# Product of w3 and w_out started with four row blocks on four accumulators, with another order of loads and a pace taken from what is left

## Chip, cores and metric

The kernel runs on one core of one Trainium2 chip. The metric is the device time of one execution in microseconds (us). Inputs are what the reference's `setup_inputs` draws; arrays stay in HBM until the kernel loads them.

## What is computed

```python
attn_out = softmax(rmsnorm(q) @ rmsnorm(k).T / 8) @ v      # 4 batches, 12 heads, 448 rows, 64 columns
x = attn_out.transpose(0, 2, 1, 3).reshape(1792, 768)
h = (x @ w1) * (x @ w2) @ w3                               # w1, w2: 768 x 1024; w3: 1024 x 1024
x = h @ w_out                                              # w_out: 1024 x 768
h = x @ w_in                                               # w_in: 768 x 2048
x = (h * clip(h + 3, 0, 6) / 6) @ w_out2                   # w_out2: 2048 x 768
```

The two products with w3 and w_out in a row have no nonlinear step between them, so the kernel multiplies w3 by w_out once, at its start, and the first block's last two products become one with the 1024 x 768 result.

## The kernel before

The program has three stages that overlap.

1. **Attention.** Heads are taken in 24 pairs, six pairs to a batch. A main loop of about 216 steps (eight steps to a pair) issues, in each step, one score product (two reduced-precision fp32 products of 448 columns, L627 and L628), its scaling and maximum on VectorE (L634), the exponential of the step before on ScalarE (L646), four transposes of an older step (L653), their copies into high and low parts (L662 on ScalarE, L672 on VectorE), and the product of transposed probabilities with V (L701 in fp32 for the first two pairs, L705 and L706 after them). L627 occurs 192 times and serves here as the step's mark.
2. **Filler.** Into each step `fill(us, aux)` puts other products worth `us` of TensorE time, taken from the generator `products()`: first `wprime()` (the product of w3 and w_out), then for each of the four batches `layer1` (L391, L396) and `layer2` (L88 to L90). `rate(t)` gives the share for step `t`. If a product's operands are not prepared the generator yields `None`, and the step goes on without it.
3. **The second block** (w_in, w_out2), a long stretch of products from L1242 and L1304, starts when the filler has ended.

`wprime()` computes 8 x 2 x 8 products of 128 x 384: for row block `a` of w3 (8), half `n` of w_out's columns (2) and inner block `c` (8). One accumulator (one PSUM bank) gathers the eight products of one `(a, n)`; `evac` copies it into a high part on ScalarE and a low part on VectorE and stores six small pieces to HBM, where `layer2` reads them back. Accumulators come from `bank(tag)`: four tags, `s` (scores), `t` (transposes), `v` (product with V) and `f` (filler), with two banks each.

The weights arrive as 64-bit floats, in half blocks: 512 KB for a half row block of w3 (kind `a`, 512 columns), 384 KB for a half block of w_out (kind `c`) and of the first layer's weights (kind `l`). All go through four `raw` buffers. `convert` makes fp32 of one: two ScalarE instructions (L148, L149) and one on VectorE (L151). A converted w3 half takes one of eight `w3` buffers, which are given back by `W["free"]` after the products of the second column half. The list `order` in `open_wprime` says in which order the half blocks are loaded and converted; `Prep` converts them one after another, up to three us' worth in each step, and no further than the buffers reach. Before the main loop the first twelve are converted, between the loads and first steps of the attention, and `fill(8.0, 0.0)` issues eight us of products.

The program is written in this order and a scheduler then places the instructions on each engine. All loads and stores go through SP's queue, in order. `issue_after` ties a load or a filler to an older instruction.

## Time and profile before

| | us |
|---|---|
| runs shown | 1142.69, 1149.24, 1151.27 |
| their median | 1149.24 |
| the profiled execution | 1141.81 |
| its span, first to last instruction | 1140.0 |

The rows further down come from the profiled execution. Times in it count from its first instruction. A timeline row gives the start, the time from the first of its merged instructions to the end of the last, the engine, the line, the operation, the tiles (written <- read) and how many there are; in brackets stands the engine's idle time before it with what ended it. An fp32 product shows as two records, a reduced-precision one as one. A product's record lasts longer than the distance to the next one's start, since products are pipelined. A row of the windows gives a stretch, its length, then for each engine its busy time with the number of instructions in brackets, at the end the granted clock of TensorE as a share of full speed, the mean busy share of the 16 DMA engines, and what they moved. A row of the waits gives the total, the number and the longest. A row of groups gives count, busy time and mean duration in ns, and the idle time before. "PE" is TensorE, "PEld" its weight loads, "DVE" VectorE, "ACT" ScalarE, "POOL" GpSimd.

### The profile page before, as it was taken

The page shows a single profiled execution, that of the slowest core. Times are in us where ns is not written, and L with a number is a line of the kernel's source. Part 1 is how long each engine was busy: PE and PEld are TensorE (multiplying, and loading weights), DVE is VectorE, ACT ScalarE, POOL GpSimd, SP SyncE. Part 2 cuts the span into 40 slices and gives each one's busy share as a digit, 9 for nine tenths or more (in the row PEclk, how much of TensorE's full clock was granted, in tenths as well). Part 3 has the DMA queues.
Part 4 walks back from the last instruction along what each step waited for, and adds up shares of the span by engine and source line. Part 5 has one row for each costly group of instructions (what it writes and reads, how often), then busy time and mean ns, then how long its engine had stood idle before and what let it go on. Part 6 is the DMA issues. An engine that isn't in the chain of part 4 may idle for free.

```text
span 1140.0 us, 17361 instructions
## 1 busy us (share of the span) xinstructions
PE 1103.1 (97%) x5483; PEld 944.0 (83%) x5483; DVE 850.8 (75%) x1927; ACT 812.4 (71%) x1729; POOL 177.9 (16%) x156
## 2 busy tenths in 40 slices
PE   5999999999999999999999999999999999999998
PEld 3545666788887888888888899899989989999998
DVE  5757988779866888778753225999988998887764
ACT  6989778899758878787754433766666776666764
POOL 1133223554322213221102000000000000000000
PEclk9999999999999999999999999999999999999999
DMA  8999655689889988997789998665469955434972
GB/s 267 331 317 342 213 171 164 243 293 377 272 279 316 308 295 269 336 342 253 232 287 324 382 362 299 217 214 200 164 228 362 389 172 168 153 117 160 335 264 74
DMA packets 109660, 299.04 MB, mean 262 GB/s; under 512 B 13280, under 2 KB 46048, under 8 KB 109568
## 3 DMA queue, kind: packets, MB, share of 16 engines
q1 hardware_dynamic: 109568, 297.93, 76.2%
q8 instruction: 43, 0.70, 0.3%
q14 instruction: 49, 0.40, 0.1%
HBM read 230.61 MB, written 67.27 MB: 261 GB/s over the span
## 4 chain that ended last, share of the span: by engine, by line
PE 60%; ACT 7%; DMA 7%; DVE 3%; issue 2%; POOL 0%; SPq 0%; ACTq 0%; POOLq 0%; DVEq 0%
PE acc L1304 17%; PE bank L391 10%; PE sB L1242 8%; PE sA L1242 8%; PE bank L396 5%; DMA rsb<-rsd 2%; PE bank L653 2%; ACT PP L646 1%; PE bank L88 1%; PE bank L89 1%; PE bank L90 1%; PE bank L627 1%; PE bank L628 1%; PE bank L706 1%; DMA raw<-in_wo_dram 1%
## 5 line engine op out<-in xcount | busy, mean ns | idle before, releaser
L1304 PE MATMUL acc<-g,wt 128*128 128x448 f32 x1008 | 211.7, 366 | 1.2 <-ACT g L1192 1.0
L1304 PEld LDWEIGHTS acc<-g,wt 128*128 128x128 f32 x1008 | 188.9, 188 | 17.7 <-ACT g L1192 1.9
L391 PE MATMUL bank<-xhl,ws 128*128 128x448 f32 x768 | 180.5, 367 | 1.6 <-ACT bs L367 1.3
L391 PEld LDWEIGHTS bank<-xhl,ws 128*128 128x128 f32 x768 | 143.5, 188 | 15.1 <-ACT bs L367 1.8
L634 DVE CUSTOM_DVE_ANT_0 PP<-bank,rb,rq 112x448 f32<-112x448 f32 x192 | 128.7, 675 | 27.4 <-PE bank L628 21.1
L646 ACT ACTIVATE PP<-PP,mx 112x448 f32<-112x448 f32 x192 | 127.5, 665 | 28.1 <-DVE mx L641 24.3
L1242 PE MATMUL sA<-xo,wt 128*128 128x448 f32 x504 | 112.0, 366 | 1.1 <-ACT u L1253 1.1
L1242 PE MATMUL sB<-xo,wt 128*128 128x448 f32 x504 | 112.2, 367 | 0.8 <-ACT u L1253 0.6
L252 PE MATMUL bank<-woh,w 128*128 128x384 f32 x256 | 97.6, 509 | 14.6 <-DVE woh L151 10.9
L1242 PEld LDWEIGHTS sB<-xo,wt 128*128 128x128 f32 x504 | 94.4, 188 | 9.9 <-ACT u L1253 1.9
L1242 PEld LDWEIGHTS sA<-xo,wt 128*128 128x128 f32 x504 | 94.6, 188 | 9.6 <-ACT u L1253 1.5
L662 ACT ACTIVATE xh<-bank 128x448 fp32r<-128x448 f32 (+1 forms) x156 | 83.1, 539 | 24.6 <-PE bank L653 20.5
L653 PEld LDWEIGHTS bank<-ident,PP 112*128 112x128 f32 x672 | 78.8, 141 | 23.9 <-issue 6.1
L1011 DVE TENSOR_TENSOR wt<-wf,wt 128x384 fp32r<-128x384 f32 x160 | 87.3, 555 | 15.1 <-ACT wt L1010 14.9
L672 DVE TENSOR_TENSOR xl<-bank,xh 128x448 fp32r<-128x448 f32 x142 | 87.4, 617 | 11.5 <-ACT xh L662 10.1
L653 PE MATMUL bank<-ident,PP 112*128 112x112 f32 x672 | 94.1, 261 | 1.5 <-DVE xl L672 1.1
L396 PE MATMUL bank<-xhl,ws 128*128 128x448 f32 x384 | 94.5, 366 | 0.0
L252 PEld LDWEIGHTS bank<-woh,w 128*128 128x128 f32 x256 | 48.9, 196 | 43.7 <-DVE woh L151 13.4
L148 ACT ACTIVATE raw<-raw 128x384 f32<-128x384 f32 (+1 forms) x112 | 63.8, 569 | 28.6 <-DMA raw<-in_wo_dram 11.6
L1010 ACT ACTIVATE wt<-wf 128x384 fp32r<-128x384 f32 x160 | 80.4, 517 | 4.8 <-PE acc L1304 2.7
L151 DVE SCALAR_TENSOR_TENSOR raw<-raw 128x384 int32<-128x384 int32 x80 | 48.9, 613 | 46.0 <-ACT raw L149 38.8
L627 PE MATMUL bank<-K,Q 128*112 128x448 f32 x192 | 77.7, 407 | 1.5 <-DVE mx L634 1.4
(134 smaller groups left out, 2110.3 us busy)
## 6 DMA issues: line engine op xcount, KB each, us to landing
ws<-w12d SPq DMA_DIRECT2D x48, 768.0 KB, 6.2
ws<-wpd SPq DMA_DIRECT2D x32, 768.0 KB, 6.5
wf<-wfd SPq DMA_DIRECT2D x56, 384.0 KB, 5.6
raw<-in_wo_dram SPq DMA_DIRECT2D x44, 384.0 KB, 5.8
td<-G SPq DMA_DIRECT2D x32, 448.0 KB, 2.5
G<-td SPq DMA_DIRECT2D x32, 448.0 KB, 6.2
raw<-in_w_dram SPq DMA_DIRECT2D x32, 384.0 KB, 6.9
w12d<-ws SPq DMA_DIRECT2D x16, 768.0 KB, 5.9
```

The source lines that it names most:

```text
L252: nc.tensor.matmul(ps[:, :NH], W["w3"][a, c // 4][:, cs], W["woh"][c, n], start=c == 0, stop=c == M1 - 1)
L391: nc.tensor.matmul(ps[:, :S], w[:, 0, ks], x[:, y, :], start=k == 0 and y == 0, stop=False)
L396: nc.tensor.matmul(ps[:, :S], w[:, 1, ks], L["xhl"][i][:, 0, :], start=False, stop=k == KD - 1)
L627: nc.tensor.matmul(ps[:CP, :S], qs, k1[:, j, :], start=True, stop=False)
L634: anchors[8 * i + s].append(nc.vector.tensor_tensor_reduce(out=T["PP", i][:, c, sl], in0=ps[:CP, :S], in1=T["rb", i][:, sl], op0=ALU.mult, ...
L646: anchors[8 * i + s].append(nc.scalar.activation(v, v, AF.Exp, bias=T["m", i][:, 8 + s : 9 + s], accum_out=T["sum", i][:, s : s + 1]))
L653: nc.tensor.transpose(ps[:, c * CP : c * CP + CP], src[:, c, kb * P : kb * P + P], ident[:CP, :CP])
L662: nc.scalar.activation(hi, ps, AF.Copy)
L672: nc.vector.tensor_sub(lo, ps, hi)
L1011: nc.vector.tensor_sub(t[:, 1, :], src, t[:, 0, :])
L1242: mm = nc.tensor.matmul(ps[:, :S], w[:, a, ks], x[:, c, :], start=first and k == 0 and n == 0, stop=k == KD // 2 - 1 and n == 2, skip_grou ...
L1304: nc.tensor.matmul(ps, w[:, y, ns], x[:, z, :], start=first and a == 0, stop=end and a == 2, skip_group_check=h in "674")
```

## The change

The first pass takes four row blocks of w3 with the first half of w_out's columns on four accumulators, two of them with tag `f` and two with tag `v`; two passes of two row blocks follow with the second half; the other four row blocks stay as they were. The load order brings the halves of row blocks 2 and 3 ahead. During `wprime` the rate is the product's remaining time over the steps left to step 58, at least 4.0 us over them, in place of 1.3 us per step, and `spent` counts the filler from the start.

```diff
-        halves = [(a, h) for a in range(2, M1) for h in range(2)]
-        order = [("a", 0, 0), ("c", 0, 0), ("a", 1, 0)] + [("c", c, 0) for c in range(1, 4)] + [("a", 0, 1), ("a", 1, 1)]
+        halves = [(a, h) for a in range(4, M1) for h in range(2)]
+        order = [("a", 0, 0), ("c", 0, 0), ("a", 1, 0)] + [("c", c, 0) for c in range(1, 4)]
+        order += [("a", 2, 0), ("a", 3, 0)] + [("a", a, 1) for a in range(4)]
         order += [("c", c, 0) for c in range(4, M1)] + [("c", c, 1) for c in range(M1)]
...
-        for group in [(0, 1)] + [(a,) for a in range(2, M1)]:
-            for n in range(2):
-                acc = [bank("f") for _ in group]
-                for c in range(M1):
-                    for a, ps in zip(group, acc):
-                        while not ready(a, n, c):
-                            yield None
-                        mul(a, n, c, ps)
-                        yield 0.73
-                    if n == 1 and c % 4 == 3:
-                        W["free"] += len(group)
+        passes = [((0, 1, 2, 3), 0), ((0, 1), 1), ((2, 3), 1)] + [((a,), n) for a in range(4, M1) for n in range(2)]
+        for group, n in passes:
+            acc = [bank("fv"[z // 2]) for z in range(len(group))]
+            for c in range(M1):
                 for a, ps in zip(group, acc):
-                    later(evac, a, n, ps)
+                    while not ready(a, n, c):
+                        yield None
+                    mul(a, n, c, ps)
+                    yield 0.73
+                if n == 1 and c % 4 == 3:
+                    W["free"] += len(group)
+            for a, ps in zip(group, acc):
+                later(evac, a, n, ps)
...
             state["debt"] -= c
-            if "pool" in L:
-                state["spent"] += c
+            state["spent"] += c
...
     def rate(t):
         if "pool" not in L:
-            return 1.3, 3
+            return max(2 * M1 * M1 * 0.73 - state["spent"], 4.0) / max(8 * HP + 10 - t, 4), 3
         if L["cur"] < 8:
             return 2.5, 4
-        left = (B - 1) * (2 * M1 * KD * 3 + KD * M1 * 3) * 0.189 - state["spent"]
+        left = 2 * M1 * M1 * 0.73 + (B - 1) * (2 * M1 * KD * 3 + KD * M1 * 3) * 0.189 - state["spent"]
         return max(left - 25.0, 0.0) / max(8 * NP + 14 - t, 1), 2
```

What the scheduler makes of it, first on SP's queue after the load of the first pair's K. `raw<-in_w3t_dram` is a half row block of w3, `raw<-in_wo_dram` a half block of w_out; before:

```order
L99 DMA kr<-in_kT_dram 128x896
L99 DMA raw<-in_w3t_dram 128x1024 x2
L99 DMA raw<-in_wo_dram 128x768 x4
L99 DMA qr<-in_qT_dram 128x896
L99 DMA kr<-in_kT_dram 128x896
L99 DMA raw<-in_wo_dram 128x768 x3
```

and after the change:

```order
L99 DMA kr<-in_kT_dram 128x896
L99 DMA raw<-in_w3t_dram 128x1024 x6
L99 DMA qr<-in_qT_dram 128x896
L99 DMA kr<-in_kT_dram 128x896
L99 DMA raw<-in_wo_dram 128x768 x3
```

Six half blocks of w3 stand in a row where two stood, and the second pair's q and k follow six weight loads as before, with larger loads among them.

On TensorE, around the second four inner blocks (`w_` and a number are w3 halves, each number another buffer; L252 of before is L253 of after); before, two row blocks:

```order
L653 MATMUL bank<-ident,PP 128x112 x2
L252 MATMUL bank<-woh,w_190 128x384
L252 MATMUL bank<-woh,w_196 128x384
L627 MATMUL bank<-K,Q 112x448
L628 MATMUL bank<-K,Q 112x448
```

and after the change, four:

```order
L628 MATMUL bank<-K,Q 112x448
L253 MATMUL bank<-woh,w_206 128x384
L253 MATMUL bank<-woh,w_212 128x384
L253 MATMUL bank<-woh,w_218 128x384
L253 MATMUL bank<-woh,w_242 128x384
L653 MATMUL bank<-ident,PP 128x112 x4
```

Each block of w_out is now followed by four products in place of two.

On TensorE, around the first product with V (L701); before, behind the 16th product of w3 and w_out:

```order
L628 MATMUL bank<-K,Q 112x448
L653 MATMUL bank<-ident,PP 128x112 x4
L701 MATMUL bank<-xh,vo 64x448
L627 MATMUL bank<-K,Q 112x448
L628 MATMUL bank<-K,Q 112x448
```

and after the change, behind the 46th:

```order
L253 MATMUL bank<-woh,w_206 128x384
L253 MATMUL bank<-woh,w_212 128x384
L701 MATMUL bank<-xh,vo 64x448 x3
L253 MATMUL bank<-woh,w_206 128x384
L253 MATMUL bank<-woh,w_212 128x384
L653 MATMUL bank<-ident,PP 128x112 x4
L687 MATMUL bank<-xh,vo 64x448 x2
```

The first product with V has moved behind 30 more products of the filler, and three of them now follow each other.

## Rows read from the trace of the kernel before

**Rows 1.** The page: busy time of each engine, share, instructions.
```profile
PE 1103.1 (97%) x5483; PEld 944.0 (83%) x5483; DVE 850.8 (75%) x1927; ACT 812.4 (71%) x1729; POOL 177.9 (16%) x156
```

**Rows 2.** Windows: busy us of PE, PEld, DVE, ACT, POOL; clock, DMA, GB/s.
```profile
0.00:25.20 25.20, 12.05 (x32) 6.08 (x33) 13.31 (x21) 15.73 (x24) 3.30 (x8) 1.00 0.91 286
25.20:67.00 41.80, 38.05 (x162) 21.96 (x160) 28.57 (x88) 39.67 (x91) 7.14 (x7) 1.00 0.96 303
67.00:130.00 63.00, 60.83 (x240) 36.42 (x241) 44.71 (x116) 56.33 (x124) 21.42 (x19) 1.00 0.94 320
130.00:195.00 65.00, 65.00 (x314) 45.75 (x312) 54.81 (x158) 50.48 (x115) 17.40 (x15) 1.00 0.51 157
195.00:241.00 46.00, 42.72 (x222) 35.85 (x222) 36.52 (x91) 40.62 (x94) 26.74 (x23) 1.00 0.77 261
241.00:298.00 57.00, 57.00 (x310) 49.42 (x309) 48.12 (x119) 52.35 (x117) 25.89 (x23) 1.00 0.95 331
298.00:370.00 72.00, 69.33 (x368) 61.23 (x368) 50.83 (x141) 50.31 (x116) 18.86 (x16) 0.98 0.88 290
```

**Rows 3.** Waits of TensorE between 25.2 and 130 us.
```profile
PE bank L252 <- DVE wst L245: 1.5, 1, 1.5
PE bank L705 <- ACT xh L662: 1.3, 1, 1.3
...
PE bank L628 <- POOL K L608: 0.7, 1, 0.7
```

**Rows 4.** Timeline of TensorE, pieces from 25 to 573 us.
```profile
41.91 0.96 PE L701 MATMUL bank<-xh,vo 128*64 128x448 f32 x2 [0.53 <-DMA vo<-in_v_dram]
...
62.98 0.43 PE L627 MATMUL bank<-K,Q 128*112 128x448 f32 x1
...
66.95 5.40 PE L252 MATMUL bank<-woh,w 128*128 128x384 f32 x16 [1.50 <-DVE wst L245]
72.18 0.55 PE L653 MATMUL bank<-ident,PP 112*128 112x112 f32 x4
...
199.22 0.36 PE L628 MATMUL bank<-K,Q 128*112 128x448 f32 x1
199.42 0.97 PE L391 MATMUL bank<-xhl,ws 128*128 128x448 f32 x4
...
208.56 0.37 PE L627 MATMUL bank<-K,Q 128*112 128x448 f32 x1
...
369.84 0.37 PE L627 MATMUL bank<-K,Q 128*112 128x448 f32 x1
...
572.73 0.36 PE L627 MATMUL bank<-K,Q 128*112 128x448 f32 x1
```

**Rows 5.** ScalarE between 25 and 130 us by form: count, busy us, mean ns.
```profile
L646 ACT ACTIVATE PP<-PP,mx 112x448 f32<-112x448 f32 x36 | 24.2, 675 | 2.2 <-DVE mx L641 2.2
L148 ACT ACTIVATE raw<-raw 128x384 f32<-128x384 f32 x22 | 12.5, 570 | 3.7 <-DMA raw<-in_w_dram 3.7
```

**Rows 6.** DMA issues between 25 and 75 us: count, KB each, us to landing.
```profile
raw<-in_wo_dram SPq DMA_DIRECT2D x10, 384.0 KB, 7.7
```

**Rows 7.** Timeline of ScalarE: four conversions.
```profile
32.95 0.56 ACT L149 ACTIVATE raw<-raw 128x384 int32<-128x384 uint16 x1
...
62.68 0.67 ACT L148 ACTIVATE raw<-raw 128x512 f32<-128x512 f32 x1 [1.21 <-DMA raw<-in_w3t_dram]
...
64.58 0.56 ACT L148 ACTIVATE raw<-raw 128x384 f32<-128x384 f32 x1 [0.68 <-DMA raw<-in_w_dram]
65.04 0.53 ACT L149 ACTIVATE raw<-raw 128x384 int32<-128x384 uint16 x1
...
80.23 0.55 ACT L148 ACTIVATE raw<-raw 128x384 f32<-128x384 f32 x1 [3.00 <-DMA raw<-in_w_dram]
80.69 0.55 ACT L149 ACTIVATE raw<-raw 128x384 int32<-128x384 uint16 x1
```

**Rows 8.** The page, part 5: weight loads of the products of w3 and w_out.
```profile
L252 PEld LDWEIGHTS bank<-woh,w 128*128 128x128 f32 x256 | 48.9, 196 | 43.7 <-DVE woh L151 13.4
```

## Prediction, made before the changed kernel was run

> **What bounds the kernel now.** The page comes first: TensorE is busy 97% of the span, VectorE and ScalarE three quarters of it [rows 1]. A share over 1140 us says little about a change that sits in the first tenth, so the windows by stage come next [rows 2]. Up to 25.2 us (the first score) every engine waits for the first loads and TensorE works 12 us; the change leaves the order of that stretch alone. From 25.2 to 67 us, the head of the attention loop, TensorE is busy 38.05 of 41.80 us, ScalarE 39.67 of 41.80, and the DMA share is 0.96: three resources are near their end at once. From 67 to 130 us TensorE idles 2.2 us, from 130 to 195 us (the rest of the w3 x w_out product) not at all, then 3.3 us around the start of layer 1 and 2.7 us near 350 us. All idle time of TensorE between 25.2 and 370 us is 11.9 us, 1.0% of the span: an ideal rearrangement of everything that the change touches would win that much.
>
> Third, the waits of TensorE between 25.2 and 130 us [rows 3]: seven kinds and 5.6 us in all, three of them shown. The largest is 1.5 us at 66.95 us, where the third accumulator pass waits for the evacuation of the pass before it. No single wait governs the head, and the granted clock is 1.00 in every window here except 0.98 in one [rows 2], so nothing is to be had from the clock.
>
> Fourth, unit prices. Eight fp32 products of 128x384 (16 records) start at 66.95 us and the next instruction at 72.18 us: 0.65 us each [rows 4]. A 448-column product in the reduced format starts 0.20 us after the one before it (199.22 and 199.42 us) [rows 4]. The product of w3 and w_out is 8 x 2 x 8 = 128 such fp32 products, 83 us of TensorE whatever the order.
>
> **What the change does to the work.** It neither removes nor adds arithmetic: 128 products, 32 loads and conversions, 16 evacuations, 96 small stores stay. It moves. Counted in the two orders at the same score instruction: before the 19th score, which comes at 62.98 us now [rows 4], TensorE has 32 of the 128 products behind it in the old order and 48 in the new (16 x 0.65 = 10.4 us more). The lead shrinks to 4 us at the 25th score, since the old order catches up there with a block of products, stands at 4 to 8 us up to the 67th, at 11 us at the 73rd (208.56 us), where the new order has begun layer 1 a little earlier, at 3 us at the 121st (369.84 us) and at 1.2 us at the last (572.73 us) [rows 4]. So the whole change is an advance of 4 to 11 us of TensorE work, lent early and repaid mostly between the 73rd and the 121st score, where the rate, which now counts from what is left, hands out some 8 us less over 48 scores.
>
> **Term 1, the head (a gain).** Moving work earlier pays only where TensorE would have idled. Idle time from 25.2 to 67 us is 3.75 us [rows 2], and 2.17 us more to 130 us: the gain of the head cannot exceed 5.9 us. It need not reach it, since the products need converted weights. The new first pass wants twelve conversions before its first 32 products, then the four c blocks left, then eight second halves of w_out. In ScalarE's order the 24th weight half-block is converted after 51.0 us of ScalarE work from the start of the program, in the order of before after 51.4 us (sums of start-to-start times of its forms, a little below the means in [rows 5], since neighbours overlap). The old 24th was converted by ScalarE at 65.57 us (65.04 and 0.53) [rows 7], so the new 24th is due at about 65.2 us, plus 0.55 us on VectorE. It is the one that the 47th and 48th products need. TensorE has 37.4 us of work from the first score to that place by the prices above, so it could be there at 62.6 us; it will wait until about 65.8. The old program reaches the same amount of work 2.6 us behind 66.95, at 69.5 us. The difference, 3.7 us, is what the head can win by this count. Against it stand two new exposures. The loads of a2 and a3 are brought ahead, so that six w3 half-blocks of 512 KB go out in a row and the second pair's q and k queue behind them on SP; TensorE already waits 0.7 us for that K now [rows 3]. And two of the four accumulators lie in the banks that the attention's P x V uses, so the first P x V, at 41.91 us in the old timeline [rows 4], stands behind 46 products instead of 16 and waits for two evacuations; queued behind it on TensorE are the 47th and 48th product and the transposes that its three buffers of copied probabilities hold up, so ScalarE's copies and the later scores wait with them. I charge 0.5 us for both together and take -3.2 us, with the ends -5.9 (all idle time of the stretch goes) and +11 us. The upper end is the case that loads set the pace: a weight half-block lands 7.7 us after its issue [rows 6] and four are in flight, so they cannot come faster than one per 1.9 us; the twelve of the old order behind the twelfth, which ScalarE finished at 33.51 us, came at 2.7 us each, two of the last after waits for their load of 1.21 and 0.68 us, and the four behind them, to 81.24 us, at 3.9 us each with a wait of 3.00 us [rows 7]. At 3.9 us each from the twelfth on, the new 24th would be converted at 80.3 us and the 47th product come at 80.9, 11.4 us after the old time.
>
> **Term 2, the repayment (a loss).** Between the 73rd and 121st score (208.56 to 369.84 us of the old run) TensorE gets about 8 us less filler. Where TensorE sets the pace the loop gets shorter by as much and nothing is lost. Where ScalarE or VectorE set it, TensorE idles. ScalarE is busy 52.35 of 57.00 us from 241 to 298 us and 50.31 of 72.00 us from 298 to 370 us [rows 2]. Squeezing the first of these by 5% takes ScalarE from 92 to 97%: still under one, but with so little room single waits appear. The ends are 0 (ScalarE keeps up) and +8 us (none of the removed filler shortens the loop). I take +1.0 us, near the first end, since at 92% TensorE had no idle time at all from 241 to 298 us [rows 2].
>
> **Term 3, the seam to layer 1 (nothing).** The new pace ends the product at about the 58th score, but layer 1 needs all six head pairs of the first batch, the last of which comes out at the 63rd step. The gap is covered by the attention alone, as the old program had it between the 65th and 73rd score; I count 21.5 us of TensorE work in twelve scores now against 22.6 before in the corresponding twelve, so the thin stretch moves and does not grow. The same holds for the evacuations (16 pairs on ScalarE and VectorE) and stores.
>
> **The sum.** -3.2 + 1.0 = -2.2 us. The profiled execution took 1141.81 us; the median of the runs shown is 1149.24, and the run that was profiled is a low one. -2.2 us on the profile is 1139.6; on the scale of the median, which the forecast is for, 1147.0 us. The measurement of this kernel tells about 1% (11.4 us) from no change; this forecast lies well within it.
>
> **A rule weighed against the rows.** In the head TensorE's weight loads are busy 21.96 of 41.80 us, 53%, while its products are busy 91% [rows 2]. By the products the stretch is nearly full; in the eight back-to-back products above each 0.65 us holds two records with one weight load apiece, and the loads' mean over all such products is 196 ns, so loads fill under 61% of a stretch that has no gap at all [rows 4, 8]. The Trainium skill, Perfetto Trace Analysis, Identifying the Most-Contended Engine, says that matmul busy time is not a good measure of headroom because matmuls are pipelined, and that the share of weight loads is better. By that rule nearly half of the head were free, the 10.4 us moved into it would cost nothing there, and the time would be 1149.24 - 10.4 = 1138.8 us, near the first rival. The trace speaks against it for this stretch: fp32 products hold TensorE for 0.33 us per load.
>
> **Rivals.**
> First, *the head has room*: TensorE's busy time in the head hides pipeline bubbles, the 16 products moved up fit in them, nothing is lost later, and the 2.2 us idle between 67 and 130 us go too, since the products there no longer wait for an evacuation or a block: 1149.24 - 10.4 - 2.2 = 1136.6 us. For it: VectorE works only 28.57 of 41.80 us there, and a busy TensorE is not TensorE at its peak. Against: total idle time of 3.75 us, ScalarE at 95% and DMA at 0.96, which have to bring the same blocks first [rows 2]. It needs the 24th block well before 60 us. Chance 0.13, of which 0.10 with more than 1%.
> Second, *the advance is lent, not won* (the other side): the 10 us are put where TensorE is already full, the attention's P x V falls behind because of the shared banks, and the lent 8 us are then missing where ScalarE paces the loop. Place: 208 to 370 us and the first P x V; price +8 (repayment) and +4 (the middle between the head's two outer values, -3.2 and +11.4), 12 us: 1161.2 us. It decides from the point at which ScalarE's share from 241 to 298 us reaches 100%. For it: 92% there. Against: the total of filler is equal at the 192nd score, and TensorE had no idle time in that window. Chance 0.17, of which 0.13 with more than 1%.
> Third, *it does nothing*: layer 1 cannot begin before the first batch is out, blocks come no faster, TensorE is full either way: 1149.2 us. Chance 0.26. My forecast holds 0.44.
>
> **How the numbers follow.** Faster by over 1%: 0.11 (the first rival's 0.10 and a little of the forecast's tail); slower by over 1%: 0.14; within: 0.75. The range reaches from 1135 us (the first rival and 4 us of the spread of the runs) to 1160 us (the second almost to its price), which leaves out under 2 in 10.
>
> **What would show it.** Right: in the new trace the 47th product near 66 us, the 19th score later than 63 us (about 70) but with about 10 us more products behind it; TensorE's idle time from 25 to 130 us at 2 to 4 us instead of 5.9; the scores near 370 us back within 3 us of their old times; the last score within 4 us of 572.73 us. Wrong in the head, if the first P x V or a product of the second halves waits over 3 us, with raw weight blocks as the releaser of ScalarE. Wrong in the middle, if TensorE idles over 3 us between 241 and 298 us with ScalarE's work behind the waits. Right for the first rival, if the score that stood at 298.24 us comes 8 us or more earlier.

## The result and the profile after

The changed kernel takes 1154.03 us, the kernel before 1145.86 us beside it (medians of 21 runs each); the ratio is 1.0078 with a 95% interval of 1.0060 to 1.0097. It is slower by 0.8%. The forecast was 0.2% faster, and the interval excludes that.

The profiled execution took 1156.38 us, its span 1154.6 us against 1140.0. Line numbers from the product on are one higher than before (L252 is L253, L391 is L392). First the busy line of the page, which answers to [rows 1], and from part 5 the weight loads, which answer to [rows 8]:

```profile
PE 1111.0 (96%) x5483; PEld 949.8 (82%) x5483; DVE 854.0 (74%) x1927; ACT 812.9 (70%) x1729; POOL 177.1 (15%) x156
...
L253 PEld LDWEIGHTS bank<-woh,w 128*128 128x128 f32 x256 | 51.2, 204 | 43.7 <-DVE woh L151 13.3
```

The same instructions, 7.9 us more busy time on TensorE and 6.7 us more idle time. The windows by stage say where, columns as in [rows 2]:

```profile
25.20:67.00 41.80, 39.88 (x157) 25.35 (x156) 29.24 (x79) 37.85 (x84) 7.63 (x6) 0.96 0.90 286
67.00:130.00 63.00, 57.97 (x224) 32.34 (x223) 42.34 (x110) 52.72 (x117) 19.27 (x18) 0.96 0.91 305
130.00:195.00 65.00, 64.05 (x301) 44.55 (x300) 53.96 (x152) 49.04 (x112) 19.51 (x17) 0.98 0.57 179
195.00:241.00 46.00, 43.57 (x228) 37.22 (x227) 34.30 (x85) 36.66 (x84) 19.27 (x18) 0.96 0.54 171
241.00:298.00 57.00, 52.46 (x268) 44.20 (x268) 45.46 (x110) 49.48 (x111) 27.98 (x24) 0.97 0.97 317
298.00:370.00 72.00, 68.52 (x364) 59.26 (x363) 52.94 (x141) 53.43 (x118) 19.66 (x17) 0.96 0.94 315
```

Idle time of TensorE over these six is 18.4 us (11.9 before), and the clock stands below 1.00 in each of them, where before it did in one. Narrow windows show the form: the clock is not a little lower, it is halved for short stretches (of the two levels, 1.2 GHz instead of 2.4):

```profile
40.00:43.40 3.40, 3.40 (x6) 1.80 (x6) 2.20 (x8) 3.40 (x11) 0.00 (x0) 0.50 1.05 325
125.30:132.10 6.80, 6.01 (x12) 3.71 (x12) 6.59 (x19) 1.14 (x3) 1.96 (x3) 0.50 0.99 312
207.20:210.60 3.40, 3.40 (x10) 3.01 (x11) 3.34 (x8) 0.54 (x1) 0.00 (x0) 0.50 0.77 252
289.10:292.50 3.40, 3.27 (x9) 2.63 (x10) 3.10 (x4) 2.87 (x8) 3.40 (x4) 0.51 0.99 398
364.20:371.00 6.80, 6.34 (x19) 5.34 (x20) 5.73 (x14) 2.87 (x6) 1.57 (x2) 0.50 0.63 205
```

That is 23.8 us, with TensorE busy for 22.4 of them: at full speed that work would have taken half, 11.2 us less (an estimate, and an upper bound on what the clock cost there). The kernel before had one such stretch in this part, read from its windows:

```profile
346.00:350.00 4.00, 1.68 (x9) 1.22 (x7) 1.15 (x2) 3.96 (x8) 2.21 (x2) 1.00 0.94 285
350.00:354.00 4.00, 3.64 (x14) 2.80 (x14) 2.81 (x9) 3.09 (x7) 0.00 (x0) 0.57 0.99 386
```

It came behind four microseconds in which TensorE was busy for 1.7. In the new kernel, too, waits stand ahead. Its waits of TensorE from 25 to 130 us (answering to [rows 3]):

```profile
PE bank L627 <- DVE mx L634: 2.4, 3, 1.4
PE bank L705 <- ACT xh L662: 1.9, 1, 1.9
PE bank L653 <- ACT xh L662: 1.7, 1, 1.7
```

and its timeline (answering to [rows 4]):

```profile
38.15 0.43 PE L627 MATMUL bank<-K,Q 128*112 128x448 f32 x1 [1.40 <-DVE mx L634]
...
39.77 4.54 PE L253 MATMUL bank<-woh,w 128*128 128x384 f32 x8 [0.44 <-DVE mx L641]
...
45.04 2.76 PE L253 MATMUL bank<-woh,w 128*128 128x384 f32 x8
...
65.46 2.47 PE L701 MATMUL bank<-xh,vo 128*64 128x448 f32 x6
67.86 1.56 PE L253 MATMUL bank<-woh,w 128*128 128x384 f32 x4
...
75.18 0.43 PE L627 MATMUL bank<-K,Q 128*112 128x448 f32 x1
...
287.49 1.49 PE L392 MATMUL bank<-xhl,ws 128*128 128x448 f32 x6 [2.51 <-ACT ws L339]
...
289.90 2.61 PE L392 MATMUL bank<-xhl,ws 128*128 128x448 f32 x6
```

The same four products of w3 and w_out (x8) take 4.54 us at 39.77 and 2.76 us at 45.04; the same six of layer 1 take 1.49 us right behind a wait of 2.51 us and 2.61 us shortly after it. 67.86 us is the 47th product, 75.18 us the 19th score.

Stretches of the clock don't belong to pieces of work. The same score in both programs does: below, TensorE's windows between the 25th, 49th, 73rd and 121st score, first before (93.16, 153.28, 208.56, 369.84 us), then after.

```profile
93.16:153.28 60.12, 57.95 (x261) 38.65 (x260) 51.78 (x139) 52.43 (x117) 18.94 (x18) 1.00 0.76 253
153.28:208.56 55.28, 54.24 (x269) 40.48 (x268) 46.97 (x136) 45.23 (x102) 20.33 (x17) 1.00 0.58 186
208.56:369.84 161.28, 156.36 (x831) 135.53 (x830) 122.59 (x309) 129.74 (x294) 62.74 (x54) 0.99 0.88 298
```

```profile
95.78:163.42 67.64, 64.30 (x271) 42.07 (x270) 52.95 (x144) 53.74 (x122) 19.67 (x18) 0.95 0.68 225
163.42:228.28 64.86, 61.48 (x302) 47.04 (x301) 51.54 (x139) 48.06 (x110) 24.66 (x22) 0.97 0.52 157
228.28:387.14 158.86, 150.85 (x792) 130.32 (x791) 119.93 (x302) 127.25 (x287) 58.52 (x51) 0.97 0.94 313
```

What a stretch holds of filler differs, so it has to be taken off: products of w3 and w_out at 0.65 us, those of the layers at 0.20 us [rows 4], counted in TensorE's order. What is left, the "rest", is the attention's own time with every wait and every slow clock in it.

| between scores | before: length - filler = rest | after | difference of the rest | rest of before in e1, e5, e6 |
|---|---|---|---|---|
| 1 and 25 | 67.9 - 31.8 = 36.1 | 70.5 - 35.7 = 34.7 | -1.4 | 36.8, 36.7, 38.4 |
| 25 and 49 | 60.1 - 28.6 = 31.5 | 67.6 - 31.9 = 35.8 | +4.3 | 31.7, 32.6, 29.6 |
| 49 and 73 | 55.3 - 24.8 = 30.5 | 64.9 - 28.4 = 36.5 | +6.0 | 30.6, 30.6, 30.6 |
| 73 and 121 | 161.3 - 92.6 = 68.7 | 158.9 - 84.8 = 74.1 | +5.4 | 65.9, 67.5, 65.2 |
| 121 and 192 | 202.9 - 113.4 = 89.5 | 205.0 - 111.6 = 93.4 | +3.9 | 95.1, 92.4, 91.3 |

The last score comes 19.4 us later (592.17 against 572.73), and 4.8 us of that are regained behind it. The spans of these two profiles lie 14.6 us apart, the medians only 8.2: the profiled run of before is a low one of its kernel, that of after one above its median, so the differences in the table are those of this pair and together too large. How firm a row is, the last column tells, from three more profiles of the same attention (e1 below is the kernel before once more, e5 and e6 change only its second block). The third row repeats within 0.1 us, the others within 2 to 6. So +6.0 us from the 49th to the 73rd score is the firm one; the first, second and fourth row after lie outside all four values of before as well, the fifth does not.

### The profile page after: what moved, and what is told of

Same layout as the page of the kernel before. It is cut to its first block, busy times and chain, and to the rows that moved or that the text cites. A ratio compares the mean times of both kernels' runs of the same rounds, so it can differ in the third digit from the quotient of the medians.

```text
span 1154.6 us, 17369 instructions
## 1 busy us (share of the span) xinstructions
PE 1111.0 (96%) x5483; PEld 949.8 (82%) x5483; DVE 854.0 (74%) x1927; ACT 812.9 (70%) x1729; POOL 177.1 (15%) x156
## 4 chain that ended last, share of the span: by engine, by line
PE 71%; ACT 11%; DMA 8%; DVE 5%; issue 3%; POOL 1%; SPq 0%; ACTq 0%; DVEq 0%; POOLq 0%
PE acc L1304 17%; PE bank L392 9%; PE sB L1242 8%; PE sA L1242 8%; PE bank L397 5%; PE bank L253 4%; PE bank L653 3%; PE bank L88 3%; PE bank L90 3%; PE bank L89 3%; ACT PP L646 2%; DMA raw<-in_wo_dram 2%; DMA nat<-in_nat_dram 2%; PE bank L627 2%; PE bank L628 2%
## 5 line engine op out<-in xcount | busy, mean ns | idle before, releaser
L392 PE MATMUL bank<-xhl,ws 128*128 128x448 f32 x768 | 183.2, 371 | 4.6 <-ACT ws L339 2.5
L392 PEld LDWEIGHTS bank<-xhl,ws 128*128 128x128 f32 x768 | 144.9, 190 | 19.2 <-ACT ws L339 3.6
L634 DVE CUSTOM_DVE_ANT_0 PP<-bank,rb,rq 112x448 f32<-112x448 f32 x192 | 128.8, 675 | 28.0 <-PE bank L628 26.2
L253 PE MATMUL bank<-woh,w 128*128 128x384 f32 x256 | 100.2, 525 | 14.0 <-DVE woh L151 11.0
L662 ACT ACTIVATE xh<-bank 128x448 fp32r<-128x448 f32 (+1 forms) x156 | 82.9, 537 | 34.1 <-PE bank L653 32.6
L397 PE MATMUL bank<-xhl,ws 128*128 128x448 f32 x384 | 96.6, 375 | 0.1
L253 PEld LDWEIGHTS bank<-woh,w 128*128 128x128 f32 x256 | 51.2, 204 | 43.7 <-DVE woh L151 13.3
L397 PEld LDWEIGHTS bank<-xhl,ws 128*128 128x128 f32 x384 | 74.3, 195 | 7.8 <-POOL ws L341 0.7
```

Source lines behind the costliest of these rows:

```text
L253: nc.tensor.matmul(ps[:, :NH], W["w3"][a, c // 4][:, cs], W["woh"][c, n], start=c == 0, stop=c == M1 - 1)
L392: nc.tensor.matmul(ps[:, :S], w[:, 0, ks], x[:, y, :], start=k == 0 and y == 0, stop=False)
L397: nc.tensor.matmul(ps[:, :S], w[:, 1, ks], L["xhl"][i][:, 0, :], start=False, stop=k == KD - 1)
L634: anchors[8 * i + s].append(nc.vector.tensor_tensor_reduce(out=T["PP", i][:, c, sl], in0=ps[:CP, :S], in1=T["rb", i][:, sl], op0=ALU.mult, ...
L662: nc.scalar.activation(hi, ps, AF.Copy)
```

## The experiments

Theories at the start: the new pace costs (by waits that it opens), the new load order costs (by the blocks that come late), or the four accumulators do (by the shared banks). "Ratio" is to the kernel before on the same chip, with its 95% interval; "clock" is the mean granted clock over the runs.

| run | what it is | us (runs) | ratio | clock |
|---|---|---|---|---|
| e1_before_again | before | 1145.98 (12) | 1.0002 [0.9979, 1.0025] | 0.997 |
| e2_pace_only | before, new pace | 1153.05 (6) | 1.0078 [1.0047, 1.0108] | 0.991 |
| e3_old_pace | after, old pace | 1149.74 (12) | 1.0035 [1.0009, 1.0061] | 0.994 |
| e4_two_acc | after, two accumulators | 1162.73 (6) | 1.0150 [1.0121, 1.0179] | 0.986 |
| e8_order_alone | new load order alone | 1143.50 (10) | 0.9997 [0.9968, 1.0026] | 0.992 |
| e13_early_dense | new pace to step 43, old end | 1152.25 (12) | 1.0047 [1.0023, 1.0070] | 0.994 |
| e14_late_dense | old pace to step 39, new end | 1147.14 (12) | 1.0007 [0.9986, 1.0027] | 0.993 |
| e15_rate115 | before, 1.15 us a step | 1146.65 (11) | 1.0026 [0.9999, 1.0053] | 0.995 |
| e16_rate145 | before, 1.45 us a step | 1154.93 (5) | 1.0100 [1.0068, 1.0133] | 0.992 |
| e17_rate16 | before, 1.6 us a step | 1158.85 (5) | 1.0121 [1.0084, 1.0157] | 0.990 |
| e18_rate18 | before, 1.8 us a step | 1155.68 (5) | 1.0094 [1.0062, 1.0126] | 0.990 |

**Which part.** The kernel before once more, for the spread of the measurement itself:

> The kernel before, unchanged, for the clock of its runs. Theory C (clock): the time of a run follows the granted clock; the changed kernel's 21 runs have a mean clock of 0.991 and a slope of about -1155 us per unit. Then this kernel's runs have a mean clock of 0.996 to 0.999, and the 8 us between the kernels are 0.006 to 0.007 of clock. Rival (stalls alone): the mean clock is 0.991 to 0.994 here too, and the 8 us come from TensorE idling longer.

Measured 1.0002, with a mean clock of 0.997, inside what theory C had.

The pace without the rest, in the kernel before:

```diff
-            if "pool" in L:
-                state["spent"] += c
+            state["spent"] += c
...
-            return 1.3, 3
+            return max(2 * M1 * M1 * 0.73 - state["spent"], 4.0) / max(8 * HP + 10 - t, 4), 3
```

> The kernel before with the new pace alone (rate from what is left, spent counted from the start); two accumulators and the old load order stay. From the 31st score on its filler stands where the changed kernel's does. Theory P (pace): the thinner filler after the 73rd score brings stalls and half-clock stretches, and this kernel is slower than before by 5 to 10 us, mean clock 0.990 to 0.993. Theory H (head: four accumulators, shared banks, load order): within 2 us of before, clock as before.

Measured 1.0078 with a clock of 0.991, a loss as large as that of the whole change, as theory P had it. The reverse, the changed kernel with `return 1.3, 3`:

> The changed kernel with the old pace of 1.3 us per step; four accumulators and the new load order stay. From the 31st score on its filler stands where the kernel before has it. Theory P (pace): within 3 us of before, clock as before. Theory H (head): slower than before by 5 to 10 us, with stalls and half clock before 130 us.

1.0035: about half of the loss goes, half stays, which neither theory expected. The first pass as two passes of two accumulators each, with the new order and pace, and the same with the old pace:

```diff
-        passes = [((0, 1, 2, 3), 0), ((0, 1), 1), ((2, 3), 1)] + ...
+        passes = [((0, 1), 0), ((2, 3), 0), ((0, 1), 1), ((2, 3), 1)] + ...
```

> The changed kernel with its load order and pace, but the first pass cut into two passes of two row blocks, so that no accumulator lies in the banks of the product with V. Theory P (pace): slower than before by 5 to 10 us like the changed kernel. Theory H in the form that the shared banks are the cause: within 3 us of before. In the form that the load order is the cause: like the changed kernel, with the loss before 130 us.

> The new load order alone: old pace, and two accumulators at a time, none of them in the banks of the product with V. Theory O (the load order costs: the second pair's K comes later behind six large loads, and without the eight products of row blocks 2 and 3 TensorE waits for it): slower than the changed kernel at the old pace (1149.7 us) by 3 to 8 us, a wait of 4 to 5 us for K near 39 us with half clock behind it. Theory B (the shared banks cost): faster than 1149.7, 1146 to 1148 us.

With the old pace the load order costs nothing on the whole (0.9997), with the new one it costs most of all (1.0150), more than any form of the theories had. Where: up to the 25th score the rest is 53.8 us in e4 (36.1 before), with 14.6 us of idle time of TensorE in it and 13.7 us at half clock in one piece. e8 loses there too (43.3 us, 10.2 us at half clock near 36 us), as theory O expected, and makes it good between the 73rd and the 121st score (60.8 us against 68.7). Both have the one wait that the order explains, for the second pair's K behind six large loads in a row; first TensorE's timeline in the run with the old pace, then with the new:

```profile
38.07 1.09 PE L627 MATMUL bank<-K,Q 128*112 128x448 f32 x2 [3.76 <-ACT K L606]
```

```profile
39.05 1.09 PE L627 MATMUL bank<-K,Q 128*112 128x448 f32 x2 [4.69 <-ACT K L606]
```

Before, that wait was 0.7 us [rows 3]. So the parts don't add: pace alone +0.8%, order alone 0, four accumulators on top of the order at the old pace about +0.4% (1.0035 against 0.9997, whose intervals still touch), everything together +0.8%. At the new pace the four accumulators are a gain: 1.0078 with them, 1.0150 without.

**What a wait costs.** To price a wait and the clock behind it apart from the attention, both kernels here add 14 waits to the second block, where TensorE is otherwise full: a copy on GpSimd, then a product of 16 columns that reads it, ahead of the block's next products; the second kernel has seven more copies in each. The main part of the edit:

```diff
...
+        if kind == "P7" and j:
+            d = mp.tile([P, 64], F32, tag="stall", bufs=1, name="stall")
+            nc.gpsimd.tensor_copy(d, c[:, :64])
+            for _ in range(0):
+                nc.gpsimd.tensor_copy(d, d)
+            snap["stall"] = nc.tensor.matmul(own[:, S : S + 16], ident, d[:, :16], start=True, stop=True,
+                                             skip_group_check=True)
...
```

(`range(7)` in the long one; in the parts left out here the products that follow are issued after it. In both the added product changes the sums of the second block.)

> The kernel before with 14 short waits of TensorE in the second block, where it has no waits of its own and the granted clock is 1.00: after each of 14 products a small fp32 product of 16 columns waits for a copy by ScalarE and one small copy by GpSimd, and the next products wait behind it. Each wait should be 1 to 1.5 us. Theory C (a wait costs more than its length, since the clock falls behind it): 14 waits cost clearly more than the idle time that the profile adds, and stretches at half clock appear in the second block. Rival (a wait costs its length): the time grows by the added idle time, 15 to 20 us, and the clock there stays at 1.00.

> The same 14 waits, each longer by seven more small copies on GpSimd, some 2 to 3.5 us long. Theory C: each is followed by a stretch at half clock; the time grows by the added idle time plus about 1.7 us each, 24 us in all. Rival (a wait costs its length): by the added idle time alone, 30 to 50 us, clock 1.00. Against the short waits it tells from which length on the clock falls.

Measured: 1190.81 us (ratio 1.0422 [1.0384, 1.0459], clock 0.997) and 1257.30 us (1.1001 [1.0967, 1.1035], clock 0.968). The timeline of TensorE around one of the waits, short and then long:

```profile
750.03 0.40 PE L1262 MATMUL sB<-stall,ident 128*128 128x16 f32 x2 [1.39 <-POOL stall L1259]
750.27 2.10 PE L1242 MATMUL sA<-xo,wt 128*128 128x448 f32 x9
```

```profile
753.03 0.61 PE L1262 MATMUL sB<-stall,ident 128*128 128x16 f32 x2 [4.47 <-POOL stall L1261]
753.48 3.71 PE L1242 MATMUL sA<-xo,wt 128*128 128x448 f32 x9
```

and the windows of the long one:

```profile
740.00:750.00 10.00, 7.05 (x34) 5.84 (x32) 9.19 (x19) 5.85 (x14) 0.74 (x2) 1.00 0.43 160
750.00:757.00 7.00, 3.97 (x12) 3.58 (x13) 1.95 (x4) 0.60 (x1) 2.61 (x7) 0.56 0.81 277
```

Nine products take 2.10 us behind the short wait and 3.71 us behind the long one. Long against short, the waits of TensorE in the second block add up to 42.3 us more (78.0 against 35.7), and the time is 66.5 us longer: 24.2 us over 14 waits, 1.7 us each, are beyond the waits, and the clock fell to half at every one of the 14. (By the two profiled runs alone, whose spans lie 70.5 us apart, it is 28.2 us, 2.0 us each.) A wait can cost its own length and 1.7 to 2.0 us more. The short ones never brought that on, against theory C, though a second wait of 1.0 to 1.5 us stands a few us ahead of nearly every one of them; why the short kernel is 46 us slower than before, with 35.7 us of waits, was not taken apart further.

**Small edits around it.** Since K came late, its loads were moved ahead of two of the weight units, in the order-alone kernel (e9), in the changed one (e10) and in the one before (e11):

```diff
-        unit(6, 10)
-        unit(7, 11)
         load_q(1)
         load_k(1)
+        unit(6, 10)
+        unit(7, 11)
```

> The new load order alone (old pace, two accumulators at a time), with the second pair's q and k loaded two weight blocks earlier, since TensorE waits 3.8 us for that K near 38 us and runs at half clock for 10 us behind it. Theory C (waits cost their length and the clock behind them): the wait goes and with it half clock near 36 us, mean clock 0.995 or more, faster than without the edit (1143.5 us) by 4 to 8 us, so faster than the kernel before. Rival (the blocks of weights then come later, and TensorE waits for those instead): within 2 us of 1143.5 us.

> The changed kernel with the second pair's q and k loaded two weight blocks earlier. Theory K (the wait of 1.4 us at 38 us and the half clock at 40 us come from that K): faster than the changed kernel by 2 to 4 us, 1150 to 1152 us, no half clock at 40 us. Rival (later waits decide): within 2 us of 1154 us.

> The kernel before with the second pair's q and k loaded two weight blocks earlier, as a control: it waits 0.7 us for that K and has no half clock there. Both theories: within 2 us of before.

1141.35 us (12 runs; 0.9971 [0.9947, 0.9994], clock 0.996), 1151.13 us (10; 1.0057 [1.0029, 1.0085]) and 1147.96 us (12; 1.0030 [1.0005, 1.0055]). The first is faster than both kernels, than the one before by 0.3%: the new load order with the second pair's q and k two units earlier, two accumulators and the old pace. It is 2 us faster than e8, not the 4 to 8 us of theory C: the wait for K is down to 0.2 us, but 6.8 us at half clock still stand at 34.3 us. e10 came out where theory K had it, though its interval overlaps that of the changed kernel. In the kernel before, the control, the same move loses 0.3%.

The weights of the layers prepared one unit further ahead of their use, `AHEAD = 4` in place of 3 (L42), in the changed kernel (e7) and in e9's (e12):

> The changed kernel with layer 1's weight units prepared up to four ahead of the one in use (three before). Theory L (the first batch's weights are converted too late for a layer 1 that now starts earlier: the 2.5 us wait at 287 us and the half clock behind it): faster than the changed kernel by 3 to 6 us, 1148 to 1151 us, no wait of that kind. Rival (ScalarE is full there, so an earlier conversion delays something else): within 2 us of the changed kernel, other waits in its place.

> The new load order at the old pace with two accumulators, q and k of the second pair earlier, and layer 1's weights prepared up to four units ahead. Theory C: fewer waits at the seam to layer 1 as well, 1134 to 1139 us, mean clock 0.997. Rival: the deeper preparation takes ScalarE from the attention, as fast as without it or slower.

1150.96 us (7; 1.0063 [1.0035, 1.0091]) and 1150.58 us (12; 1.0052 [1.0024, 1.0081]): in the changed kernel it makes no difference clear of noise, e9 it makes 0.8% slower (1.0052 against 0.9971), where theory C had expected a gain. Neither helps.

**Which end of the pace.** In the kernel before, the new pace puts more products in from the 19th score on (8 more behind it at the 31st, 11 at the 49th) and finishes the product some six scores earlier. Each half alone, in the kernel before:

```diff
+            return max(2 * M1 * M1 * 0.73 - state["spent"], 4.0) / max(8 * HP + (10 if t < 44 else 18) - t, 4), 3
```

```diff
+            if t < 40:
+                return 1.3, 3
+            return max(2 * M1 * M1 * 0.73 - state["spent"], 4.0) / max(8 * HP + 10 - t, 4), 3
```

> The kernel before with the new pace up to step 43 and an end at step 66 in place of 58 behind it: its filler is 5 to 6 us ahead from the 31st to the 43rd score and where the old one's is from the 61st on. Theory S (the seam: layer 1 begun earlier, its operands not there, less filler behind it): within 3 us of before, 1143 to 1147 us. Rival D (the denser stretch itself costs, conversions and copies falling behind TensorE before 150 us): like the new pace alone, 1150 to 1155 us.

> The kernel before with the old pace up to step 39 and the new one from there: its filler is where the old one's is up to the 37th score and 11 us or more ahead at the 73rd, as with the new pace. Theory S: like the new pace alone, 1150 to 1155 us, with waits for layer 1's operands and half clock near 207 and 288 us. Rival D: within 3 us of before.

1.0047 and 1.0007: the dense start loses, the early end doesn't, as rival D had it. That spoke for the density itself, but a new interleaving of any kind might move the time by as much, as e11 and e12 did. So the density alone, with a constant rate in the kernel before (`return 1.15, 3` and so on):

> The kernel before with 1.15 us of filler per step in place of 1.3, all else as before: 6 us less of the product of w3 and w_out before the 49th score (90 products instead of 101), and its end at the 73rd score instead of the 67th. Theory 'density' (the denser the filler beside the attention's first 49 scores, the slower): under 1146 us at that place, but the product's end now falls late and starts layer 1 late, so 1143 to 1150. Theory 'any interleaving' (the time moves by up to 0.5% either way with each new order, without a direction): anything between 1140 and 1152. Alone this run tells little; it is the low end of the row of four.

> The kernel before with 1.45 us of filler per step: almost the same filler up to the 49th score as the new pace alone gave (111 products against 112), its end at the same place. Theory 'density': like the new pace alone, 1150 to 1155 us, with two or more stretches of half clock between 25 and 370 us. Theory 'any interleaving': no bond to that kernel's 1153; 1140 to 1152, as likely below 1146 as above.

> 1.6 us per step: 121 products before the 49th score, 13 us more than the kernel before, and the product ends at the 53rd. Theory 'density': slower than the kernel with 1.45, 1153 to 1158 us. Theory 'any interleaving': 1140 to 1152, without an order among the four.

> 1.8 us per step: the whole product is done by the 49th score (128 products against 101), and between the 49th and the 72nd score no filler is left that could run, so TensorE has the attention alone there. Theory 'density': the slowest of the four, 1156 to 1165 us, from the dense part and from the empty one behind it. Theory 'any interleaving': it still loses the empty stretch if ScalarE or VectorE sets the pace there, 1146 to 1156.

1.0026, then 1.0100, 1.0121 and 1.0094. All three above the old rate lose 1%, the one below it at most half a per cent: that has a direction, and "any interleaving" falls as the whole explanation. But the time does not rise on with the rate, as theory 'density' had it, and the densest kernel's trace shows that its dense stretch isn't what costs. That kernel between its 25th, 49th and 73rd score:

```profile
104.13:168.61 64.48, 64.48 (x285) 43.24 (x283) 50.09 (x137) 48.74 (x108) 17.34 (x15) 1.00 0.62 200
168.61:227.15 58.54, 51.59 (x244) 37.77 (x243) 49.00 (x137) 46.58 (x104) 24.68 (x21) 0.91 0.63 200
```

In the first stretch TensorE has no idle time and a full clock: 37.1 us of filler instead of 28.6 for 4.4 us of length, 4.1 us won. In the second 14.4 us of filler are left instead of 24.8, and it is not 10 us shorter than the 55.28 us of before but 3.3 us longer. Idle time there is 6.95 us against 1.04, and a clock of 0.91 over 58.54 us takes up to 5.3 us more (an estimate); together 11.2 of the 13.6 us by which the rest grew.

The rest between the 49th and the 73rd score, over the profiles (e5 and e6, with the attention of before, stand in the table above):

| pace | rest from the 49th to the 73rd score, us |
|---|---|
| old or thinner (before, its repetition, e15, e3, e8, e9, e11, e12) | 30.5, 30.6, 30.6, 31.3, 32.0, 31.9, 31.4, 31.9 |
| denser ahead of it (after, e2, e4, e7, e10, e13, e14, e16, e17, e18) | 36.5, 35.7, 33.9, 33.5, 34.7, 36.3, 36.7, 39.6, 42.5, 44.1 |

The two groups don't overlap, whatever load order, number of accumulators or place of K they have, and the rest is largest where the product ends soonest. In this stretch the product of w3 and w_out runs out and layer 1 begins: 27 products of the one and 36 of the other before, 16 and 90 after the change, 21 and 10 in e13, none and 72 in e18. So the densest kernel has less filler there than before, the changed one has more (28.4 us against 24.8), and what TensorE waits for differs. Its waits in this stretch, before and then after the change:

```profile
PE bank L561 <- DVE mx L641: 0.5, 1, 0.5
PE bank L627 <- DVE mx L634: 0.3, 1, 0.3
PE bank L706 <- DVE xl L672: 0.2, 1, 0.2
```

```profile
PE bank L392 <- POOL xhl L361: 1.4, 1, 1.4
PE bank L706 <- DVE mx L641: 0.8, 1, 0.8
PE bank L392 <- ACT xhl L360: 0.7, 1, 0.7
PE bank L653 <- DVE xl L672: 0.2, 1, 0.2
```

`xhl` is layer 1's operand, made by ScalarE and GpSimd from the attention's output, one head pair at a time. Layer 1 now starts at the 61st score in place of the 68th and waits for it, 2.1 us in all, with the half clock of 207.2 us behind the longer of the two. In e18 most of the waiting there is for the attention's own chain (2.9 us for ScalarE's copies `xh`, 2.3 us for VectorE's maximum L634, 0.7 us for `xhl`).

The attention's own work in the stretch is not quite the same everywhere either: TensorE has 80 transposes and 45 products with V there before, 92 and 53 in e14, 92 and 54 in e16, 76 and 42 in e18. At 0.10 and 0.20 us apiece (an estimate from their distances in the traces) e14 comes to 33.9, e16 to 36.6 and e18 to 45.1 us; the groups then reach from 29.2 to 31.0 and from 33.1 to 45.1 us and still don't overlap.

The total does not follow this row alone: e14 has 36.7 us there and is no slower than before. About 2.8 of its 6.2 us are such work moved in from other stretches. In its profile it has 29.8 us between the 25th and 49th score (31.5 before) and 65.4 between the 73rd and 121st (68.7), but these rows repeat badly, and how e14 makes good the remaining 3 us stays open.

## Why the prediction was wrong

The forecast was -2.2 us, the medians differ by +8.2 us. The range of 1135 to 1160 us held 1154.03, and "within 1%" was right; the direction was wrong, and three terms with it. The step whose failure repeats is the seam, put at nothing: the rest there grew by 6.0 us, and it is larger in all ten kernels that issue the product earlier. The gain of the head did not come, the repayment cost more than was charged, and half clock behind waits stood in no term. The new pace by itself, in the kernel before, brings a loss of the same size (e2).

**Term 1, the head, -3.2 us: failed.** Up to the 25th score the rest is 1.4 us smaller, up to the 49th 2.9 us larger (70.5 us against 67.6 to 69.3 in the four profiles of before). The idle time from 25 to 130 us, to fall from 5.9 to 2 to 4 us, is 6.95 us. The count of conversions behind it was right. The 24th weight half block was due on ScalarE at about 65.2 us; ScalarE's timeline, answering to [rows 7], has it at 64.93 and 0.54, with load waits ahead of it and behind it:

```profile
64.47 0.56 ACT L148 ACTIVATE raw<-raw 128x384 f32<-128x384 f32 x1 [1.11 <-DMA raw<-in_wo_dram]
64.93 0.54 ACT L149 ACTIVATE raw<-raw 128x384 int32<-128x384 uint16 x1
...
68.53 0.67 ACT L148 ACTIVATE raw<-raw 128x512 f32<-128x512 f32 x1 [2.70 <-DMA raw<-in_w3t_dram]
```

What failed is the sentence that TensorE "could be there at 62.6 us" and would wait for the block: it came to the 47th product at 67.86 us, behind its own waits and the half clock at 40.0 us, and behind six records of the first product with V (65.46 us). The load pace feared as the upper end (80.3 us) did not come. Nor does a wait of the first product with V, part of the 0.5 us charged, stand at 65.46 us; what the shared banks cost shows only in the comparison of e3 with e8, not clear of noise. The 19th score, foretold at about 70 us, came at 75.18.

**Term 2, the repayment, +1.0 us: mis-sized.** The 8 us less of filler between the 73rd and 121st score are there (84.8 against 92.6), and the loop got shorter by 2.4 us, not by 8: 5.4 us lost against this profile of before, 6.6 to 8.9 against the three others. The size is that of one profile: e7 and e10 take still more filler out there (78.6 and 78.0 us are left) and have a rest of 69.1 and 64.9 us. The argument "at 92% TensorE had no idle time at all" was the weak one, and the prediction's own sign for it came, over 3 us of idle time from 241 to 298 us. ScalarE did not come to 97% from 241 to 298 us but to 49.48 of 57.00 us, 87%, and TensorE idled 4.54 us all the same, the longest piece of it in one wait of 2.51 us for a weight conversion at 287.49 us, on an engine that was not full.

**Term 3, the seam, nothing: failed.** It compared sums of TensorE's work over twelve scores, found 21.5 against 22.6 us, and had the gap covered by the attention alone until the last pair is out at the 63rd step. Layer 1 started at the 61st score and waited for its operand, and the attention's chain had waits of its own. The rest from the 49th to the 73rd score grew by 6.0 us (30.5 to 36.5), and it is larger in all ten kernels that issue more of the product ahead of it. Of the 6.0 us, 2.3 are idle time of TensorE and up to 1.7 the half clock of 3.4 us; the other 2 us were not taken apart.

**The clock.** "Nothing is to be had from the clock" was true of before and left out that there was something to lose. Over the 21 runs the mean granted clock is 0.991, against 0.996 in the runs of the kernel before beside the experiments; 0.0053 of 1150 us is 6.1 us (an estimate), out of 8.9 us that the ratio gives. That the other 2.8 us are idle time is likely but not shown. Nor is the clock a cause apart from the waits: in e6 it fell at each of the 14 long ones. And it doesn't decide the time alone: e8 has 0.992 and loses nothing.

**The rivals.** "The advance is lent, not won" (1161.2 us, chance 0.17) was the nearest in mechanism: the repayment as priced, and TensorE already full when the advance was given. Its condition, ScalarE at 100%, was wrong, as was its first product with V. "It does nothing" missed the sign, and room of the kind that "the head has room" supposed shows only later: with the densest rate 4.1 us were won between the 25th and the 49th score, and lost again behind it.

**The rule on weight loads.** The rows of before spoke against it, and so do those of after: in the head the weight loads are busy 25.35 of 41.80 us, 61%, while TensorE idled 1.92 us. The Trainium skill, Perfetto Trace Analysis, Identifying the Most-Contended Engine, has headroom judged by the share of weight loads, beside the share of peak arithmetic; by the first of these 39% of the head would have been free (an estimate), and this trace disagrees.

**Open.** Between the 49th and the 73rd score, thinner filler with a late start of layer 1 (e13) and an early start of it (e14) both raise the rest; what each costs by itself was not tried. Why e13 loses 0.5% and e14 nothing, that row does not explain. Why the new load order makes the stretch from the 73rd to the 121st score shorter (60.8 us in e8 and 60.6 in e9 against 68.7 and 65.9) was not tried either, and e9's gain hangs on it.

## What to carry to other kernels

Filler taken forward changes the place where it stood: here that place became thin (e18), or the next product moved into it before its operands were ready (the changed kernel). Price that place before the one the filler goes to, between the same marks in the work and with the filler's own time taken off. A chain through several engines can stall TensorE in single waits before any engine's share comes to 100% (here with ScalarE at 87%), so "the others have 8% left" is no cover. And a wait of TensorE can have a second price, the half clock behind it, which an idle column doesn't show; read the granted clock in narrow windows.

## What the runs showed that was not expected

- Half clock came behind waits of quite different length: at 39.77 us behind 1.40 and 0.44 us with work between them, at 289.1 us behind one of 2.51 us, behind all 14 waits of 4.0 to 4.5 us in e6 and behind none of the 1.4 us waits in e5; in e9 6.8 us of it came at 34.3 us behind waits of at most 0.83 us. Length alone did not tell which.
- The same small edit has opposite signs in neighbours: q and k two units earlier bring 0.9997 to 0.9971 on the new load order and 1 to 1.0030 in the kernel before, and a deeper look-ahead costs 0.8% in e9 and nothing in the changed kernel. Differences under half a per cent between such schedules say little on the edit by itself.
